# Layer-norm rows in two halves with Newton roots on VectorE, a shift table in four pieces, and a new load order in a single-core convolution-and-MLP kernel

## The chip, the cores and the metric

The kernel runs on one core of a Trainium2 chip. The metric is the device time of one execution in microseconds (us), median of several executions. A core has TensorE (matmuls; PE in the profile, with PEld for its weight loads), VectorE (DVE), ScalarE (ACT), GpSimd (POOL), and the queues of 16 DMA engines (SP starts most loads). They run side by side and wait for each other by semaphores.

Times are compared between kernels run on the same chip in the same set, each with its own executions of the kernel before; where two sets are compared, the text says so, and the kernel before had means of 192.71 to 192.88 us in all of them. That kernel was very steady: 192.63 to 192.95 us in almost all sets (one execution of 193.43).

## The reference

Two branches share the input `q` (2048 rows of 640, bf16), and a gate per row mixes them.

```python
x = A_q                                             # [1, 2048, 640]
g = sigmoid((x * gate_w).sum(-1))                   # gate, one per row
# branch A: 4-tap causal shift of k, times v, then a long convolution along the rows
k_shift = sum over t of k_pad[:, t:t+S, :] * shift_k[:, 3-t]
kv = k_shift * v
y  = irfft(rfft(kv, 2S) * rfft(ssm_k, 2S))[:S] + kv * ssm_D
a  = q * y
# branch B: rows normalised, then an MLP that mixes along the rows
h  = (x - mean(x)) / sqrt(var(x) + 1e-5)            # per row of 640
u  = gelu(einsum("bsd,sf->bdf", h, w1) + b1)
b  = transpose(einsum("bdf,fs->bds", u, w2) + b2)
return g * a + (1 - g) * b
```

## The kernel before

The convolution is done as matrix products with sine tables. The stages that matter here, with the names that tiles have in the program:

1. TensorE transposes the filter (`wT<-ssm`) and transforms it in two blocks of 64 matmuls (`wT,FTB`), "the filter products". ScalarE drains each group of four to `C`. VectorE then combines the result ("filter mixing", `SS<-C`, `C<-C`).
2. VectorE computes mean and variance of 16 tiles of 128 rows (`stats`, `mv`), the reciprocal roots are found (`rstd`), and each tile of `X` is normalised in place.
3. The 4-tap shift of `k` is 80 small matmuls (`KF,KT`) per half against a table `KF` that GpSimd builds: "the k convolution". VectorE multiplies by `v` (`vkv`), TensorE transforms the product (`vkv,FTB`).
4. The first MLP product (`X,ring`, 384 matmuls) needs no branch A. It is the filler that TensorE takes where branch A has nothing ready; every group of it needs normalised rows. The second (`GT,W`) follows, and the inverse transform of branch A (`C,GTB` and `SS,GTB`, four times 32 matmuls) comes between its groups near the end.

The program is written as a list of operations with estimated durations. A list scheduler inside the kernel's own code decides the order on each engine before the program is built, by a priority and those estimates. On the chip the order is fixed; only the waits differ. PSUM is cut in four accumulators: at most three for branch A ("cv") and two for the MLP ("mlp").

```python
self.limit = {"mlp": 2, "cv": 3}          # of NSLOT = 4 accumulators
# ... cut ...
def ln_apply():
    ts("POOL", sd[:, :], mv[:, :, 1], 1e-5, None, ALU.add)               # var + eps
    tt("POOL", rstd[:, :], sd[:, :], V(cst, 1, [[0, 16]]), ALU.pow)      # ** -0.5
    tt("POOL", sd[:, :], sd[:, :], rstd[:, :], ALU.mult)
    for t in range(16):
        xs = X[:, t // 4, t % 4, :]
        ts("DVE", xs, xs, mv[:, t, 0:1], rstd[:, t:t + 1], ALU.subtract, ALU.mult, mode=4, extra=0.16)
# ... cut ...
            if h == 0:
                for hk in range(4):
                    for p in range(4):
                        ln_tile(hk, p)
                ln_apply()
                for g0 in (0, 10):        # the shift table, two pieces
                    tt("POOL", KF[:, g0:g0 + 10, :, :], V(cw, 7 * g0, ...), V(m32, 0, ...), ALU.mult)
                for hk in range(2):
                    k_turn(hk)            # VectorE copies a row block of k, DMA transposes it
                mixing(C[0], SS, 0, fine=True)
```

Of the kernel before, what the change touches and what calls it, by code (L numbers as in the profile page):

```python
# [308 lines left out]
class _Op:  # L309
    __slots__ = ("eng", "dur", "emit", "prio", "idx", "ndep", "succ", "vt", "vtrole", "end", "start", "kind", "lat", "deps", "name", "after", "nafter", "asucc")  # L310

# [11 lines left out]
class _Sched:  # L323
# [29 lines left out]
    def add(self, eng, dur, emit, reads, writes, prio=None, vt=None, lat=0.0, name=""):  # L353
        op = _Op()
        op.eng, op.dur, op.emit, op.lat, op.name = eng, dur, emit, lat, name
        op.idx = len(self.ops)
        op.prio = op.idx if prio is None else prio
        op.vt = vt
        deps = set()
        self._conf(op, reads, "R", deps)  # L360
        self._conf(op, writes, "W", deps)
        if vt is not None:
            vt.left += 1
            if vt.last_pe is not None:
                deps.add(vt.last_pe)
            if eng == "PE":
                if vt.first is None:
                    vt.first = op
                vt.last_pe = op
            else:  # L370
                for d in deps:
                    if d.vt is not vt:
                        if d not in vt.first.deps:
                            vt.first.deps.add(d)
        op.deps = deps
        op.after = set()
        self._rec(op, reads, "R")
        self._rec(op, writes, "W")
        self.ops.append(op)
        return op  # L380

    def run(self):
# [12 lines left out]
        pend = {e: [] for e in engs}  # L395
        free = {e: 0.0 for e in engs}
        dma_free = 0.0
        avail = {}
# [13 lines left out]
        while started < n:  # L412
# [6 lines left out]
            for e in engs:  # L419
# [32 lines left out]
                if e in ("SP", "QA") or op.lat < 0:  # L452
                    issue = 0.1
                    s = max(t + issue, dma_free)
# [3 lines left out]
                else:  # L458
                    op.end = t + op.dur
                    free[e] = op.end  # L460
                order.append(op)
# [43 lines left out]
def _build(nc, A_q, A_k, A_v, A_shift_k, A_ssm_k, A_ssm_D, B_x, B_w1, B_b1, B_w2, B_b2, gate_w, out):  # L505
# [10 lines left out]
    with ExitStack() as es:  # L516
# [97 lines left out]
        def tt(eng, o, a, b, op, mode=2, prio=None):  # L614
            n = n_of(o)
            d = dve_dur(n, mode) if eng == "DVE" else n / 500.0 + 0.3
            return SC.add(eng, d, lambda s: T.op(eng, lambda e: e.tensor_tensor(o, a, b, op), [a, b], [o]),  # L617
                          [a, b], [o], prio=prio, name="tt")

        def ts(eng, o, a, s1, s2, op0, op1=None, mode=1, prio=None, extra=0.0):  # L620
# [4 lines left out]
            def f(e):  # L625
                if s2 is None:
                    return e.tensor_scalar(o, a, s1, None, op0=op0)  # L627
                return e.tensor_scalar(o, a, s1, s2, op0=op0, op1=op1)  # L628
            return SC.add(eng, d, lambda s: T.op(eng, f, rr, [o]), rr, [o], prio=prio, name="ts")

# [89 lines left out]
        def k_turn(hk):  # L720
            o, i = kp[hk % 2], kn[hk % 2]
            ov = o[:, :, :].rearrange("p g (q c) -> p g q c", q=4)
            iv = V(i, 0, [[32, NG], [D, 4], [1, 32]])
            SC.add("DVE", 0.75, lambda s: T.op("DVE", lambda e: e.tensor_copy(ov, iv), [i[:, :, :]], [o[:, :, :]]), [i[:, :, :]], [o[:, :, :]], prio=0, name="kperm")  # L724
            c0 = 16 + 128 * (hk % 2)
# [19 lines left out]
        x_load(0)  # L745
        dma(gwb[:, :], dr(gate_w, 0, [[0, 128], [1, D]]), 128 * 1280, chain=True)
        for hk in range(1, 4):
            x_load(hk)
        ssm_load(2)
        ssm_load(3)  # L750

        T_PI = float(np.float32(math.pi * (1.0 - 1e-6)))
        memset("DVE", cst[:, 0:1], T_PI)
        memset("DVE", cst[:, 1:2], -0.5)
        iota = lambda ap, pat, b, cm: SC.add("POOL", 0.5, lambda s: T.op("POOL", lambda e: e.iota(ap, pat, base=b, channel_multiplier=cm), [], [ap]), [], [ap])
        iota(dif[:, :], [[1, 128]], 0, -1)
# [17 lines left out]
        for hk in range(2):  # L774
            k_load(hk)
        for hk in range(4):
            w1_load(0, hk)

        vt = _VT("cv")
# [41 lines left out]

        def mixing(R, Th, Ts, fine=False, conj=False):
            def sl(h, s, n=1):
# [24 lines left out]

        def ln_apply():
            ts("POOL", sd[:, :], mv[:, :, 1], 1e-5, None, ALU.add)  # L850
            tt("POOL", rstd[:, :], sd[:, :], V(cst, 1, [[0, 16]]), ALU.pow)
            tt("POOL", sd[:, :], sd[:, :], rstd[:, :], ALU.mult)
            for t in range(16):
                xs = X[:, t // 4, t % 4, :]
                ts("DVE", xs, xs, mv[:, t, 0:1], rstd[:, t:t + 1], ALU.subtract, ALU.mult, mode=4, extra=0.16)

        srcW = lambda h: (lambda kt, p, ci: wT[:, 2 * h + kt, p, 320 * ci:320 * ci + 320])
        for h in range(2):
# [5 lines left out]
            if h == 0:  # L864
                for hk in range(4):
                    for p in range(4):
                        ln_tile(hk, p)
                ln_apply()
                for g0 in (0, 10):
                    tt("POOL", KF[:, g0:g0 + 10, :, :], V(cw, 7 * g0, [[7, 10], [1, 7], [0, 32]]), V(m32, 0, [[0, 10], [0, 7], [1, 32]]), ALU.mult)  # L870
                for hk in range(2):
                    k_turn(hk)
                mixing(C[0], SS, 0, fine=True)
            else:
                mixing(C[1], C[0], 0, conj=True)

# [276 lines left out]
```

## Time and profile before

The median is 192.79 us (three executions, 192.77 to 192.95). The profiled execution spans 190.9 us.

| stretch (us) | TensorE | what else |
|---|---|---|
| 0 to 5.34 | waits for the first filter load | |
| 14.29 to 24.55 | 64 filter products, 161 ns each | ScalarE busy 96% |
| 24.55 to 29.2 | 40 transposes, 4.65 us | ScalarE busy throughout |
| 29.2 to 41.8 | 64 filter products and 24 MLP matmuls | |
| 50.3 to 51.75 | waits 1.04 us for the product of k and v | VectorE full |
| 64.6 to 187.8 | 928 matmuls, 132.7 ns each, no gap | |
| 187.8 to 190.9 | done: tail | ScalarE, VectorE, last store |

The first two lines of the page: span and busy times of each engine, with shares and instruction counts.

```profile
span 190.9 us, 3358 instructions
...
PE 177.4 (93%) x1403; PEld 130.5 (68%) x1403; DVE 170.3 (89%) x195; ACT 116.4 (61%) x187; POOL 33.0 (17%) x29
```

TensorE's timeline of the kernel before. Columns: start (us), duration (us), engine, source line (a helper's), operation, output and inputs, shapes, count; in brackets idle time before it and who ended it.

```profile
14.29 10.29 PE L293 MATMUL pp<-wT,FTB 128*128 128x320 bf16 x64 [0.43 <-ACT wT L655]
24.55 0.45 PE L293 MATMUL pp<-ident,ssm 128*128 128x128 bf16 x5
25.15 3.96 PE L293 MATMUL pp<-ident,ssm 128*128 128x128 bf16 x35 [0.15 <-ACT C L655]
29.24 1.31 PE L293 MATMUL pp<-wT,FTB 128*128 128x320 bf16 x8
30.64 1.43 PE L293 MATMUL pp<-X,ring 128*128 128x320 bf16 x8
31.90 4.01 PE L293 MATMUL pp<-wT,FTB 128*128 128x320 bf16 x28
...
40.68 1.25 PE L293 MATMUL pp<-X,ring 128*128 128x320 bf16 x8
41.77 4.33 PE L293 MATMUL pp<-KF,KT 128*128 128x128 bf16 x80
```

Two things are to be seen. The 40 transposes have no MLP group between them, because no row is normalised before 30 us. From 30.64 us on three groups of eight MLP matmuls (`X,ring`) stand inside the second filter block (the first and the last are shown).

Why the rows come at 30 us is in GpSimd's timeline and in VectorE's:

```profile
13.65 7.84 POOL L617 TENSOR_TENSOR KF<-cw,m 128x2240 bf16<-128x2240 bf16 x2 [5.40 <-DVE mv L847]
25.60 1.39 POOL L627 TENSOR_SCALAR sd<-mv 128x16 f32<-128x16 f32 x1 [4.11 <-DVE mv L847]
27.07 2.94 POOL L617 TENSOR_TENSOR rstd<-sd,cst 128x16 f32<-128x16 f32 x1
30.09 0.22 POOL L617 TENSOR_TENSOR sd<-sd,rstd 128x16 f32<-128x16 f32 x1
```

```profile
23.17 1.48 DVE L617 TENSOR_TENSOR SS<-C 128x2560 bf16<-128x2560 bf16 x1
...
30.05 5.79 DVE L628 TENSOR_SCALAR X<-X,mv,rstd 128x640 bf16<-128x640 bf16 x16 [3.19 <-POOL rstd L617]
```

The table runs first, then the roots (1.39 + 2.94 + 0.22 us), and VectorE idles 3.19 us for them. (The page names `mv` as what the table waited for, only because an `mv` ended just before. The table reads `cw` and `m`; ScalarE's drain of `cw` ended at 13.51 us.) The end of TensorE's timeline:

```profile
175.68 4.51 PE L293 MATMUL pp<-SS,GTB 128*128 128x320 bf16 x32
180.02 7.77 PE L293 MATMUL pp<-GT,W 128*128 128x320 bf16 x56
```

After the last inverse product (`SS,GTB`) 56 MLP matmuls follow. The wait of TensorE for the product of k and v, from the list of waits (engine, who waited for whom: total us, times, longest):

```profile
PE pp L293 <- DVE vkv L617: 1.0, 1, 1.0
```

### The profile page before, as it was taken

To read this page: it belongs to the slowest core of one execution; us is meant where nothing else is said; L and a number is where in the kernel's file an instruction comes from. 1 tells how busy PE (TensorE), PEld (TensorE's weight loads), DVE (VectorE), ACT (ScalarE), POOL (GpSimd) and SP (SyncE) were. 2 spreads that over 40 slices of the span, in tenths; PEclk is the share of its full clock that TensorE was granted. 3 is DMA by queue.
4 is the path that set the end of the run, shared out by engine and by line. 5 is a ranking of instruction groups with operands and counts; after the bars stand their busy time and mean duration, and the time that the engine had idled before them with its cause. 6 is when DMAs were issued, how large, how long until landed. Compare 5 with 4: busy or idle time off the path is not lost.

```text
span 190.9 us, 3358 instructions
## 1 busy us (share of the span) xinstructions
PE 177.4 (93%) x1403; PEld 130.5 (68%) x1403; DVE 170.3 (89%) x195; ACT 116.4 (61%) x187; POOL 33.0 (17%) x29
## 2 busy tenths in 40 slices
PE   0749989999799999999999999999999999999993
PEld 0536555678566976767777777888888777886782
DVE  7999967999999799999999969999999958999451
ACT  4799997889599999998411221131322467516632
POOL 2619563600006300010012102250000000000000
PEclk9999999999999999999999999999999999999999
DMA  5999999993799999994368914999947903210222
GB/s 155 327 412 378 372 238 230 307 407 136 136 181 306 250 232 306 272 329 96 59 138 251 231 27 138 272 208 195 263 136 224 367 18 137 72 69 2 72 103 103
DMA packets 37296, 38.93 MB, mean 204 GB/s; under 512 B 15644, under 2 KB 32673, under 8 KB 37281
## 3 DMA queue, kind: packets, MB, share of 16 engines
q1 hardware_dynamic: 34464, 32.15, 54.7%
q0 software_dynamic: 2752, 6.55, 18.6%
q8 instruction: 11, 0.18, 0.4%
q14 instruction: 5, 0.03, 0.0%
q10 hardware_dynamic: 64, 0.01, 0.0%
HBM read 25.87 MB, written 2.62 MB: 149 GB/s over the span
## 4 chain that ended last, share of the span: by engine, by line
PE 71%; DVE 19%; DMA 4%; POOL 2%; issue 2%; SPq 0%; ACT 0%; DVEq 0%
PE pp L293 71%; DVE stats L845 6%; DMA X<-in_A_q_dram 4%; DVE X L628 3%; DVE SS L617 3%; DVE C L617 2%; DVE kp L724 2%; POOL rstd L617 2%; DVE vkv L617 1%; DVE mv L847 1%; POOL sd L627 1%; SPq L267 0%; ACT O L655 0%; DVE O L617 0%; DVEq L187 0%
## 5 line engine op out<-in xcount | busy, mean ns | idle before, releaser
L293 PE MATMUL pp<-X,ring 128*128 128x320 bf16 x384 | 54.0, 299 | 0.1
L293 PE MATMUL pp<-GT,W 128*128 128x320 bf16 x384 | 52.8, 299 | 0.0
L617 DVE TENSOR_TENSOR C<-C 128x2560 bf16<-128x2560 bf16 (+1 forms) x28 | 48.9, 1769 | 1.2 <-ACT C L655 1.1
L293 PEld LDWEIGHTS pp<-GT,W 128*128 128x128 bf16 x384 | 43.5, 113 | 8.9 <-ACT cgb L655 0.2
L293 PEld LDWEIGHTS pp<-X,ring 128*128 128x128 bf16 x384 | 37.1, 98 | 15.4 <-DVE X L628 0.7
L655 ACT ACTIVATE C<-pp 128x640 bf16<-128x640 f32 x64 | 39.6, 741 | 4.4 <-PE pp L293 4.3
L655 ACT ACTIVATE O<-pp,c,omg 128x640 bf16<-128x640 f32 (+1 forms) x17 | 14.5, 853 | 32.9 <-PE pp L293 32.9
L655 ACT ACTIVATE GT<-pp,cc 128x640 bf16<-128x640 f32 x12 | 9.6, 797 | 22.1 <-PE pp L293 21.9
L617 DVE TENSOR_TENSOR tm<-C,C 128x2560 bf16<-128x2560 bf16 (+2 forms) x12 | 20.2, 1708 | 1.9 <-DMA C<-tm 1.9
L293 PE MATMUL pp<-wT,FTB 128*128 128x320 bf16 x128 | 19.6, 310 | 0.6 <-ACT wT L655 0.4
L655 ACT ACTIVATE cgb<-pp,gg 128x640 bf16<-128x640 f32 x16 | 12.7, 793 | 7.7 <-PE pp L293 7.7
L293 PEld LDWEIGHTS pp<-wT,FTB 128*128 128x128 bf16 x128 | 11.5, 101 | 8.0 <-ACT C L655 2.3
L617 DVE TENSOR_TENSOR C<-tm 128x2560 bf16<-128x2560 bf16 (+1 forms) x12 | 15.0, 1263 | 0.1
L293 PE MATMUL pp<-ident,ssm 128*128 128x128 bf16 x80 | 8.8, 265 | 6.6 <-DMA ssm<-in_A_ssm_k_dram 5.3
L262 POOL DMA_DIRECT2D C<-C x6 | 7.5, 1407 | 36.0 <-DVE C L617 36.0
L845 DVE BATCH_NORM_STATS2 stats<-X 128x6 f32<-128x320 bf16 x32 | 13.4, 463 | 0.3 <-DMA X<-in_A_q_dram 0.3
L293 PE MATMUL pp<-C,GTB 128*128 128x320 bf16 x96 | 13.6, 299 | 0.0
L293 PEld LDWEIGHTS pp<-ident,ssm 128*128 128x128 bf16 x80 | 6.3, 127 | 9.1 <-DMA ssm<-in_A_ssm_k_dram 5.3
L293 PEld LDWEIGHTS pp<-C,GTB 128*128 128x128 bf16 x96 | 9.0, 98 | 4.0 <-ACT O L655 0.2
L655 ACT ACTIVATE gq<-gq 128x640 bf16<-128x640 bf16 x16 | 11.8, 756 | 0.0
L617 DVE TENSOR_TENSOR tm<-C,SS 128x5120 bf16<-128x5120 bf16 x4 | 11.2, 2817 | 0.0
L655 ACT ACTIVATE wT<-pp 128x640 bf16<-128x640 f32 x16 | 10.1, 812 | 1.1 <-PE pp L293 1.1
(64 smaller groups left out, 177.2 us busy)
## 6 DMA issues: line engine op xcount, KB each, us to landing
ring<-in_B_w_dram SPq DMA_DIRECT2D x12, 512.0 KB, 10.3
W<-in_B_w_dram SPq DMA_DIRECT2D x8, 768.0 KB, 7.3
C<-C POOLq DMA_DIRECT2D x6, 640.0 KB, 10.5
ssm<-in_A_ssm_k_dram SPq DMA_DIRECT2D x4, 640.0 KB, 9.1
X<-in_A_q_dram SPq DMA_DIRECT2D x4, 640.0 KB, 9.5
kn<-in_A_k_dram SPq DMA_DIRECT2D x4, 640.0 KB, 9.2
out_dram<-O SPq DMA_DIRECT2D x7, 320.0 KB, 2.3
vkv<-in_A_v_dram SPq DMA_DIRECT2D x2, 640.0 KB, 4.7
```

The lines of the kernel that those rows point to most:

```text
L262: ins = engobj.dma_start(out_ap, in_ap, accum_op=ALU.add, max_dma_last_dim=2560)
L293: ins = self.nc.tensor.matmul(ps_ap, lhsT=lhsT, rhs=rhs, start=start, stop=stop, skip_group_check=True)
L617: return SC.add(eng, d, lambda s: T.op(eng, lambda e: e.tensor_tensor(o, a, b, op), [a, b], [o]), [a, b], [o], prio=prio, name="tt")
L627: return e.tensor_scalar(o, a, s1, None, op0=op0)
L628: return e.tensor_scalar(o, a, s1, s2, op0=op0, op1=op1)
L655: return T.op("ACT", lambda e: e.activation(o, src, func, **kw), rr + [src], ww)
L724: SC.add("DVE", 0.75, lambda s: T.op("DVE", lambda e: e.tensor_copy(ov, iv), [i[:, :, :]], [o[:, :, :]]), [i[:, :, :]], [o[:, :, :]], prio ...
L845: SC.add("DVE", 0.38, (lambda o, i: lambda s: T.op("DVE", lambda e: e.bn_stats(o, i), [i], [o]))(o, i), [i], [o])
L847: SC.add("DVE", 0.12, (lambda o, i: lambda s: T.op("DVE", lambda e: e.bn_aggr(o, i), [i], [o]))(o, i), [i], [o])
```

## The change

Its intent: normalise the first eight tiles as soon as their statistics are there, so that MLP matmuls can fill the holes in the first 30 us; take the roots away from GpSimd, where the table stands in the way, and compute them on VectorE by a bit trick and three Newton steps; cut the table in four pieces; give the filter mixing a lower priority; load two pieces of `w1` early. The estimates of the scheduler are corrected as well: operations of VectorE and GpSimd that share a port lock each other in the model.

```diff
+        op.lock = eng == "POOL"            # in the scheduler: such operations wait for one another
+                    if op.lock:
+                        op.end += max(port["POOL" if e == "DVE" else "DVE"] - t, 0.0)
+                        port[e] = op.end
# ... cut: durations of GpSimd operations, lock set on copies and tensor operations ...
         x_load(0)
-        dma(gwb[:, :], ...)
-        for hk in range(1, 4):
-            x_load(hk)
+        x_load(1)
+        w1_load(0, 0)
         ssm_load(2)
         ssm_load(3)
+        x_load(2)
+        w1_load(0, 1)
+        x_load(3)
# ... cut ...
-        def ln_apply():
-            ts("POOL", sd[:, :], mv[:, :, 1], 1e-5, None, ALU.add)
-            tt("POOL", rstd[:, :], sd[:, :], V(cst, 1, [[0, 16]]), ALU.pow)
-            tt("POOL", sd[:, :], sd[:, :], rstd[:, :], ALU.mult)
-            for t in range(16):
+        def ln_scale(a, b):
+            v, y, z, m_ = sd[:, a:b], rstd[:, a:b], gth[:, a:b], mv[:, a:b, 1]
+            # ... cut: yi, vi are y, v read as int32 ...
+                op(lambda e: e.tensor_scalar(v, m_, 1e-5, None, op0=ALU.add), [m_], v)
+                op(lambda e: e.tensor_scalar(yi, vi, 1, None, op0=ALU.logical_shift_right), [vi], yi)
+                op(lambda e: e.tensor_scalar(yi, yi, -1.0, float(0x5F3759DF), op0=ALU.mult, op1=ALU.add), [yi], yi)
+                for _ in range(3):
+                    op(lambda e: e.scalar_tensor_tensor(out=z, in0=y, scalar=-0.5, in1=y, op0=ALU.mult, op1=ALU.mult), [y], z)
+                    op(lambda e: e.tensor_tensor(z, z, v, ALU.mult), [z, v], z)
+                    op(lambda e: e.scalar_tensor_tensor(out=y, in0=z, scalar=1.5, in1=y, op0=ALU.add, op1=ALU.mult), [z, y], y)
+                op(lambda e: e.tensor_tensor(v, v, y, ALU.mult), [v, y], v)
+            return SC.add("DVE", 1.5, emit, [m_], [v, y, z], prio=0, name="rstd")
+        def ln_apply(a, b):
+            for t in range(a, b):
# ... cut ...
+        MIXP = 330
+        LNG = ((0, 8), (8, 16))
+        KFP = (0, 5, 10, 15)
# ... cut ...
+                for a, b in LNG:
+                    for t in range(a, b):
+                        ln_tile(t // 4, t % 4)
+                    ln_scale(a, b)
+                    ln_apply(a, b)
+                for g0 in KFP:              # the shift table, four pieces
+                    tt("POOL", KF[:, g0:g0 + 5, :, :], ...)
-                mixing(C[0], SS, 0, fine=True)
+                mixing(C[0], SS, 0, fine=True, prio=MIXP)
```

More of the change, by code (lines that the diff above doesn't have):

```diff
@@ L309 @@
 class _Op:
-    __slots__ = ("eng", "dur", "emit", "prio", "idx", "ndep", "succ", "vt", "vtrole", "end", "start", "kind", "lat", "deps", "name", "after", "nafter", "asucc")
+    __slots__ = ("eng", "dur", "emit", "prio", "idx", "ndep", "succ", "vt", "vtrole", "end", "start", "kind", "lat", "deps", "name", "after", "nafter", "asucc", "lock")
 class _VT:
@@ L396, in run @@
         free = {e: 0.0 for e in engs}
+        port = {"DVE": 0.0, "POOL": 0.0}
         dma_free = 0.0
@@ L452, in run @@
                 if e in ("SP", "QA") or op.lat < 0:
-                    issue = 0.1
+                    issue = 1.2 if e == "POOL" else 0.1
                     s = max(t + issue, dma_free)
@@ L615, in tt @@
             n = n_of(o)
-            d = dve_dur(n, mode) if eng == "DVE" else n / 500.0 + 0.3
-            return SC.add(eng, d, lambda s: T.op(eng, lambda e: e.tensor_tensor(o, a, b, op), [a, b], [o]),
-                          [a, b], [o], prio=prio, name="tt")
+            d = dve_dur(n, mode) if eng == "DVE" else n / 600.0 + 0.17
+            o_ = SC.add(eng, d, lambda s: T.op(eng, lambda e: e.tensor_tensor(o, a, b, op), [a, b], [o]),
+                        [a, b], [o], prio=prio, name="tt")
+            o_.lock = True
+            return o_
+        tt_ = tt
         def ts(eng, o, a, s1, s2, op0, op1=None, mode=1, prio=None, extra=0.0):
@@ L628, in f @@
                 return e.tensor_scalar(o, a, s1, s2, op0=op0, op1=op1)
-            return SC.add(eng, d, lambda s: T.op(eng, f, rr, [o]), rr, [o], prio=prio, name="ts")
+            o_ = SC.add(eng, d, lambda s: T.op(eng, f, rr, [o]), rr, [o], prio=prio, name="ts")
+            o_.lock = eng == "POOL" or mode > 1
+            return o_
         def stt(eng, o, a, sc, b, op0, op1, acc=None, prio=None):
@@ L723, in k_turn @@
             iv = V(i, 0, [[32, NG], [D, 4], [1, 32]])
-            SC.add("DVE", 0.75, lambda s: T.op("DVE", lambda e: e.tensor_copy(ov, iv), [i[:, :, :]], [o[:, :, :]]), [i[:, :, :]], [o[:, :, :]], prio=0, name="kperm")
+            SC.add("DVE", 0.75, lambda s: T.op("DVE", lambda e: e.tensor_copy(ov, iv), [i[:, :, :]], [o[:, :, :]]), [i[:, :, :]], [o[:, :, :]], prio=0, name="kperm").lock = True
             c0 = 16 + 128 * (hk % 2)
@@ L745, in _build @@
         x_load(0)
-        dma(gwb[:, :], dr(gate_w, 0, [[0, 128], [1, D]]), 128 * 1280, chain=True)
-        for hk in range(1, 4):
-            x_load(hk)
+        x_load(1)
+        w1_load(0, 0)
         ssm_load(2)
         ssm_load(3)
+        x_load(2)
+        w1_load(0, 1)
+        x_load(3)
         T_PI = float(np.float32(math.pi * (1.0 - 1e-6)))
@@ L754, in _build @@
         memset("DVE", cst[:, 1:2], -0.5)
-        iota = lambda ap, pat, b, cm: SC.add("POOL", 0.5, lambda s: T.op("POOL", lambda e: e.iota(ap, pat, base=b, channel_multiplier=cm), [], [ap]), [], [ap])
+        iota = lambda ap, pat, b, cm: SC.add("POOL", 0.2, lambda s: T.op("POOL", lambda e: e.iota(ap, pat, base=b, channel_multiplier=cm), [], [ap]), [], [ap])
         iota(dif[:, :], [[1, 128]], 0, -1)
@@ L775, in _build @@
             k_load(hk)
-        for hk in range(4):
+        for hk in range(2, 4):
             w1_load(0, hk)
+        dma(gwb[:, :], dr(gate_w, 0, [[0, 128], [1, D]]), 128 * 1280, chain=True)
         vt = _VT("cv")
@@ L820, in fwd, with mixing, tt @@
                     act(o, two, ACT.Copy, vt=vt, name=name + "e", **kw)
-        def mixing(R, Th, Ts, fine=False, conj=False):
+        def mixing(R, Th, Ts, fine=False, conj=False, prio=None):
+            def tt(*a):
+                return tt_(*a, prio=prio)
             def sl(h, s, n=1):
@@ L847, in ln_tile, with emit, op @@
             SC.add("DVE", 0.12, (lambda o, i: lambda s: T.op("DVE", lambda e: e.bn_aggr(o, i), [i], [o]))(o, i), [i], [o])
-        def ln_apply():
-            ts("POOL", sd[:, :], mv[:, :, 1], 1e-5, None, ALU.add)
-            tt("POOL", rstd[:, :], sd[:, :], V(cst, 1, [[0, 16]]), ALU.pow)
-            tt("POOL", sd[:, :], sd[:, :], rstd[:, :], ALU.mult)
-            for t in range(16):
+        def ln_scale(a, b):
+            v, y, z, m_ = sd[:, a:b], rstd[:, a:b], gth[:, a:b], mv[:, a:b, 1]
+            yi = y.bitcast(I32)
+            vi = v.bitcast(I32)
+            def emit(s):
+                def op(fn, rr, w):
+                    T.op("DVE", fn, rr, [w])
+                op(lambda e: e.tensor_scalar(v, m_, 1e-5, None, op0=ALU.add), [m_], v)
[9 more added lines that the diff above has]
+            for t in range(a, b):
                 xs = X[:, t // 4, t % 4, :]
-                ts("DVE", xs, xs, mv[:, t, 0:1], rstd[:, t:t + 1], ALU.subtract, ALU.mult, mode=4, extra=0.16)
+                ts("DVE", xs, xs, mv[:, t, 0:1], rstd[:, t:t + 1], ALU.subtract, ALU.mult, mode=4, extra=0.16, prio=1)
+        MIXP = 330
+        LNG = ((0, 8), (8, 16))
+        KFP = (0, 5, 10, 15)
         srcW = lambda h: (lambda kt, p, ci: wT[:, 2 * h + kt, p, 320 * ci:320 * ci + 320])
@@ L864, in _build @@
             if h == 0:
-                for hk in range(4):
-                    for p in range(4):
-                        ln_tile(hk, p)
-                ln_apply()
-                for g0 in (0, 10):
-                    tt("POOL", KF[:, g0:g0 + 10, :, :], V(cw, 7 * g0, [[7, 10], [1, 7], [0, 32]]), V(m32, 0, [[0, 10], [0, 7], [1, 32]]), ALU.mult)
+                for a, b in LNG:
[4 more added lines that the diff above has]
+                for g0 in KFP:
+                    tt("POOL", KF[:, g0:g0 + 20 // len(KFP), :, :], V(cw, 7 * g0, [[7, 20 // len(KFP)], [1, 7], [0, 32]]), V(m32, 0, [[0, 20 // len(KFP)], [0, 7], [1, 32]]), ALU.mult)
                 for hk in range(2):
                     k_turn(hk)
-                mixing(C[0], SS, 0, fine=True)
+                mixing(C[0], SS, 0, fine=True, prio=MIXP)
             else:
-                mixing(C[1], C[0], 0, conj=True)
+                mixing(C[1], C[0], 0, conj=True, prio=MIXP)
         memset("POOL", KT[0][:, :, 15:16], 0.0)
```

## The prediction

> **What bounds the kernel now.** The stretches show TensorE busy 177.4 of 190.9 us; the chain of waits is 71% TensorE, one unbroken run from 51.75 to 187.8 us. From 64.6 us it takes 123.2 us for 928 matmuls (132.7 ns each): saturated, so the only gain there is having less left to do. The tail (3.1 us) and the wait for the first filter load (5.3 us) are untouched. Holes between 18 and 65 us:
> - 24.55 to 29.2: 40 filter transposes take 4.65 us (113 ns each; ScalarE drains five per 0.63 us). The short matmuls of the k convolution go at 54 ns, so 2.4 us are free.
> - 14.3 to 24.55: 64 filter matmuls at 161 ns instead of 133, again paced by ScalarE; about 0.6 us free after 20 us.
> - 29.2 to 41.8: 88 matmuls in 12.6 us, 0.85 us free.
> - 46 to 51.75: TensorE waits 1.04 us for the k·v product, which on VectorE stood behind the filter mixing.
> - 51.75 to 64.6: about 0.7 us.
>
> Sum 5 to 6 us, the ceiling. The filler is the first MLP product, which needs normalised rows, now from about 30.5 us: statistics end at 25.5 us, GpSimd then needs 1.39 + 2.94 + 0.22 us for the roots, and VectorE idles 3.2 us.
>
> **What the change does.**
> - Halves: statistics of 8 tiles, 8 x 0.86 us (8.8 to 15.7); Newton, 13 dependent small operations at an estimated 0.15 to 0.2 us (independent ones show 0.17), 2 to 2.6 us; then 8 x 0.36 us. First rows at about 18 us, half done at 21 to 24; second half at 34 to 36, as before (35.8).
> - VectorE pays two Newton chains (4 to 5 us) and saves 3.2 us of idling: about even.
> - Half the rows and two MLP accumulators give at most 32 matmuls, 4.3 us of filler: just what the holes before 34 us take.
> - The shift table on GpSimd (2 x 3.9 us from 13.65) now overlaps the normalising. The Trainium skill ("SBUF — State Buffer", on the shared port pair) says such VectorE instructions and GpSimd ones lock each other out for a whole instruction. The trace agrees: GpSimd's 16-element add took 1.39 us, ending with VectorE's 1.45 us operation. Four pieces keep each block to about 2 us.
> - With the mixing behind, k·v goes first: most of the 1.04 us goes. The last inverse products have 7.8 us of MLP matmuls behind them as slack.
> - Two weight pieces go earlier, so k and the last rows land about 2.8 us later (1 MB at 370 GB/s), at 19 to 24 us; VectorE gets to them no earlier.
>
> **Predicted time.** Of the 5 to 6 us, 3 to 4 should be won: 2 to 2.5 in the transposes and first filter products, 0.8 in the k·v wait, the rest small. 189.5 us, 8 in 10 between 187.6 and 191.5; faster by over 2% 0.32, within 2% 0.66, slower 0.02.
>
> **What would show it.** MLP matmuls in TensorE's timeline from 18 to 22 us, between transposes; the stretch of transposes over 95% useful; no wait on k·v above 0.3 us; the saturated run starting some 3 us earlier with as much left; the tail still 3.1 us; VectorE busy some 3 us more; first-half normalising instructions that last 1 to 2 us where a table piece runs.
>
> **What would make it wrong.** Table pieces that block the first half beyond 24 us; Newton steps twice as dear; MLP groups that give ScalarE, over 90% busy before 42 us, bubbles; k transposes that land late and starve the k convolution; deferred mixing that makes inverse products late near 150 or 171 us.

## The result, and the profile after

The changed kernel took 193.62 us (median of four executions), the kernel before 192.78 us. The ratio is 1.004 (95% interval 1.002 to 1.006): within 2%, but slower, where 189.5 us were predicted. Three of the four executions took 193.45 to 193.70 us. One, the profiled one, took 1038.88 us and is left out; it is told of at the end.

Because of that the profile shown is of a later execution of the same kernel (the run e9 below, 193.32 us). Its page:

```profile
span 191.5 us, 3379 instructions
...
PE 177.3 (93%) x1403; PEld 129.9 (68%) x1403; DVE 180.4 (94%) x221; ACT 116.3 (61%) x187; POOL 26.6 (14%) x28
```

TensorE's busy time is the same to 0.1 us. VectorE's went up by 10.1 us, not by some 3. VectorE's timeline where the roots are computed, and the table on GpSimd beside it:

```profile
16.04 0.94 DVE L874 TENSOR_SCALAR sd<-mv 128x8 f32<-128x8 f32 x1
17.01 1.99 DVE L875 TENSOR_SCALAR rstd<-sd 128x8 int32<-128x8 int32 x1
19.03 1.99 DVE L876 TENSOR_SCALAR rstd<-rstd 128x8 int32<-128x8 int32 x1
21.05 1.98 DVE L878 SCALAR_TENSOR_TENSOR gth<-rstd 128x8 f32<-128x8 f32 x1
23.07 0.17 DVE L879 TENSOR_TENSOR gth<-gth,sd 128x8 f32<-128x8 f32 x1
...
24.75 2.94 DVE L637 TENSOR_SCALAR X<-X,mv,rstd 128x640 bf16<-128x640 bf16 x8
```

```profile
14.88 8.13 POOL L622 TENSOR_TENSOR KF<-cw,m 128x1120 bf16<-128x1120 bf16 x4 [6.62 <-ACT cw L666]
```

This is the first thing to see. An operation on eight columns takes 0.17 us when nothing stands beside it (the fifth line). The first four took 0.94, 1.99, 1.99 and 1.98 us, and they end, one for one, as the four pieces of the table end (at 16.94, 18.97, 20.99 and 14.88 + 8.13 = 23.01 us; the fifth operation starts at 23.07). The Newton chain took 8.7 us (16.04 to 24.75) instead of the predicted 2 to 2.6. The Trainium skill ("SBUF — State Buffer", section "Who interferes with whom") says that a VectorE instruction in a two-port mode, or with two inputs in SBUF, contends with a GpSimd instruction that reads SBUF, and that the second to issue blocks fully until the first ends. The trace agrees, down to operations of eight columns. It also agrees with what the same section says of instructions outside these cases: the statistics ran at 0.46 us each beside the table, in both kernels.

VectorE's timeline of the second half:

```profile
35.87 1.48 DVE L622 TENSOR_TENSOR SS<-C 128x2560 bf16<-128x2560 bf16 x1
...
37.38 1.49 DVE L622 TENSOR_TENSOR C<-C 128x2560 bf16<-128x2560 bf16 x1
...
41.30 1.49 DVE L622 TENSOR_TENSOR SS<-C 128x2560 bf16<-128x2560 bf16 x1
42.70 2.94 DVE L637 TENSOR_SCALAR X<-X,mv,rstd 128x640 bf16<-128x640 bf16 x8
```

The second half is normalised from 42.70 to 45.6 us; before, all 16 tiles were done at 35.84. Three mixing operations stand in front, though the change wanted them behind. TensorE's timeline for the same stretch as above:

```profile
13.86 10.46 PE L293 MATMUL pp<-wT,FTB 128*128 128x320 bf16 x64
24.29 0.44 PE L293 MATMUL pp<-ident,ssm 128*128 128x128 bf16 x5
25.34 1.43 PE L293 MATMUL pp<-X,ring 128*128 128x320 bf16 x8 [0.61 <-DVE X L637]
26.60 1.00 PE L293 MATMUL pp<-ident,ssm 128*128 128x128 bf16 x15
27.44 1.25 PE L293 MATMUL pp<-X,ring 128*128 128x320 bf16 x8
...
29.76 0.47 PE L293 MATMUL pp<-ident,ssm 128*128 128x128 bf16 x5 [0.24 <-ACT wT L666]
30.36 9.67 PE L293 MATMUL pp<-wT,FTB 128*128 128x320 bf16 x64
39.99 4.33 PE L293 MATMUL pp<-KF,KT 128*128 128x128 bf16 x80
```

The first MLP group comes at 25.34 us, not at 18 to 22, after a wait of 0.61 us for rows. Two groups (16 matmuls) stand between the transposes, and none in the second filter block: the third group belongs to the same accumulator and needs the second half's rows. So the filler came earlier, but there were 16 matmuls of it before the k convolution where there had been 24. Two waits of TensorE remain:

```profile
PE pp L293 <- DVE vkv L622: 0.6, 1, 0.6
PE pp L293 <- DVE X L637: 0.6, 1, 0.6
```

And the end:

```profile
180.55 1.79 PE L293 MATMUL pp<-GT,W 128*128 128x320 bf16 x12
182.18 4.51 PE L293 MATMUL pp<-SS,GTB 128*128 128x320 bf16 x32
```

Here nothing follows the last inverse product. TensorE ends at 186.7 us, 1.1 us before the old kernel's 187.8, but the tail is 4.8 us (191.5 - 186.7) instead of 3.1 (190.9 - 187.8).

The account between the two traces: TensorE is 1.1 us ahead from 51 us on (it starts its product of k and v at 50.64 instead of 51.75, with the same work done), stays so to its end, and the tail gives back 1.7 us.

### The profile page after: what moved, and what is told of

It reads as the page before. It is cut to its first block, busy times and chain, and to the rows that moved or that the text cites. A ratio compares the mean times of both kernels' runs of the same rounds, so it can differ in the third digit from the quotient of the medians.

```text
span 1037.1 us, 3379 instructions
## 1 busy us (share of the span) xinstructions
PE 1026.6 (99%) x1403; PEld 438.7 (42%) x1403; DVE 177.1 (17%) x221; ACT 125.4 (12%) x187; POOL 27.5 (3%) x28
## 3 DMA queue, kind: packets, MB, share of 16 engines
q1 hardware_dynamic: 34464, 32.15, 10.1%
## 4 chain that ended last, share of the span: by engine, by line
PE 99%; DMA 0%; DVE 0%; ACT 0%; DVEq 0%; issue 0%
PE pp L293 99%; DMA ssm<-in_A_ssm_k_dram 0%; DVE cgb L622 0%; ACT cgb L666 0%; DVE O L622 0%; DVEq L503 0%
## 5 line engine op out<-in xcount | busy, mean ns | idle before, releaser
L293 PE MATMUL pp<-X,ring 128*128 128x320 bf16 x384 | 320.3, 1212 | 0.0
L293 PE MATMUL pp<-GT,W 128*128 128x320 bf16 x384 | 318.6, 1211 | 0.0
L293 PEld LDWEIGHTS pp<-GT,W 128*128 128x128 bf16 x384 | 123.8, 323 | 193.4 <-issue 193.4
L293 PEld LDWEIGHTS pp<-X,ring 128*128 128x128 bf16 x384 | 124.0, 323 | 189.5 <-issue 187.4
L293 PE MATMUL pp<-wT,FTB 128*128 128x320 bf16 x128 | 106.5, 1213 | 0.0
L293 PE MATMUL pp<-C,GTB 128*128 128x320 bf16 x96 | 80.4, 1209 | 0.0
L293 PE MATMUL pp<-vkv,FTB 128*128 128x320 bf16 x64 | 54.1, 1204 | 0.0
L293 PE MATMUL pp<-kv,FTB 128*128 128x320 bf16 x64 | 53.9, 1210 | 0.0
L293 PE MATMUL pp<-KF,KT 128*128 128x128 bf16 (+1 forms) x160 | 47.0, 663 | 0.0
L293 PEld LDWEIGHTS pp<-KF,KT 128*128 128x128 bf16 x160 | 43.5, 314 | 5.0 <-issue 2.1
```

The lines of the kernel that those rows point to most:

```text
L293: ins = self.nc.tensor.matmul(ps_ap, lhsT=lhsT, rhs=rhs, start=start, stop=stop, skip_group_check=True)
```

## The experiments

Two theories stood at the start. Theory L/P: the table blocks the Newton chain piece by piece (P), and VectorE's lateness sets the time (L). Rival T: TensorE is full from 64 us on and VectorE has slack, so its lateness costs nothing; then the loss has another cause. Theory E came from the first traces: the order at TensorE's end makes the tail. Theory S came later: the late second half starves the filler.

| run | what differs from the changed kernel | median us | ratio to before (95%) |
|---|---|---|---|
| first | nothing | 193.62 | 1.004 (1.002 to 1.006) |
| e0 | nothing | 194.44 | 1.008 (1.004 to 1.012) |
| e9 | nothing | 193.80 | 1.006 (1.004 to 1.007) |
| e1 | one Newton step | 192.31 | 0.998 (0.995 to 1.000) |
| e2 | table in two pieces (TensorE's order moved a little) | 194.41 | 1.009 (1.007 to 1.010) |
| e3, e11 | table behind the first half | 192.22, 192.21 | 0.998, 0.997 |
| e10 | 12 MLP matmuls last on TensorE | 193.03 | 1.001 (0.997 to 1.004) |
| e12 | as e11, inverse product last | 193.57 | 1.005 (1.003 to 1.006) |
| e16 | table behind, every order kept | 192.01 | 0.996 (0.994 to 0.997) |
| e17 | e16 and e10 together | 190.91 | 0.989 (0.988 to 0.991) |
| e13 | as e11, mixing really behind (other orders moved too) | 191.06 | 0.991 (0.989 to 0.992) |
| e4 | table behind, roots on GpSimd | 191.68 | 0.994 (0.993 to 0.996) |
| e5 | as e4, second MLP accumulator early | 195.95 | 1.015 (1.012 to 1.019) |
| e6 | load order of before | 192.12 | 0.996 (0.994 to 0.998) |
| e7 | table behind, Newton not in halves | 195.60 | 1.015 (1.012 to 1.018) |
| e8 | e4 with the load order of before | 191.55 | 0.993 (0.990 to 0.996) |
| e14 | e8 with the mixing behind | 191.80 | 0.995 (0.993 to 0.997) |
| e15 | e14 with Newton roots | 191.58 | 0.996 (0.994 to 0.998) |

All gave correct results.

### e0: the changed kernel again

No edit.

> The changed kernel unchanged, because its profiled execution took 1038.9 us with matmuls of 1.2 us each, while its three other executions took 193.45 to 193.70. Theory A (that execution was disturbed from outside the program): this look takes 193.5 us within 0.3 and its matmuls of 320 columns are back to about 0.30 us each. Theory B (the changed program has a slow mode of its own): one of its executions here again takes over 250 us. The trace should also show why it is 0.8 us slower than before and not 3.3 us faster: either TensorE fills the transposes before 29 us and loses elsewhere before 65 us, or its first MLP matmul comes later than 22 us.

Measured: 194.44 us (193.82 to 195.22), matmuls of 320 columns at 0.30 us. So the 1038.9 us were of that one execution; it did not come back in the 10 executions of e0 and e9, and the profiles above and below could be read. The expectation of 193.5 within 0.3 us missed: this kernel spreads. The traces of e0 (195.02 us) and e9 (193.32 us) show where these two differ: in e0 TensorE waited 1.25 us at 145 us for a load of `w2`, in e9 not. The first filter block took 11.6 us in e0 and 10.5 in e9, but that was nearly made up by shorter waits for VectorE after it: at the second k convolution e0 is only 0.25 us behind (61.62 against 61.37). The line of e0:

```profile
146.03 17.04 PE L293 MATMUL pp<-GT,W 128*128 128x320 bf16 x124 [1.25 <-DMA W<-in_B_w_dram]
```

### e1: one Newton step instead of three

```diff
-                for _ in range(3):
+                for _ in range(1):
```

Its result is a little less exact. The scheduler does not see inside the chain, so every engine's order stays.

> One Newton step instead of three in each half, order of everything else on every engine the same: VectorE has 12 operations of about 0.2 us less, 2.4 us in all; the result is a little less exact, on purpose. Theory L (VectorE's lateness sets the end of the changed kernel): 1 to 2.5 us faster than the changed kernel's 193.5 to 195.2, and the first MLP matmul about 1.2 us earlier, at 24.7 us. Rival T (TensorE sets the end, full from 64 us on, and VectorE has slack as the prediction held): no change within 0.4 us. The blocked steps remain: the first four Newton operations still take 0.9 + 3 x 2 us.

Measured: 192.31 us, ratio 0.998 against 1.004 to 1.008 for the changed kernel: 1.2 to 1.9 us for 12 small operations that take 2.4 us on VectorE. The first four operations were still blocked (0.88, 1.99, 1.99, 1.98 us). First MLP matmul at 25.28 us, hardly earlier, since the filter block before it ran until 25.0 in this trace; what went are the waits for rows and for the product of k and v. Rival T falls: VectorE's lateness counts. But it counts through waits of TensorE before 51 us, not at the end as theory L had it: the tail is still 4.8 us.

### e2: the table in two pieces

```diff
-        KFP = (0, 5, 10, 15)
+        KFP = (0, 10)
```

> The shift table in two pieces of about 4 us, as before, in place of four of 2 us. Theory P (each small VectorE operation waits for one whole GpSimd piece, one after another): two Newton operations of up to 4 us, chain over only when the table is done, at about 23.3 us plus the rest, first rows normalised again near 25 us and the time within 0.5 us of the changed kernel. Rival Q (the long operations are a cost of the first integer or shift operation, not of GpSimd): still three operations of 2 us each. Prediction (shorter pieces block less): four pieces would be better, so this one is 2 us or more later at the first rows.

Measured: 194.41 us, within the spread of four pieces. (The new estimates also moved a few of TensorE's groups between 65 and 81 us, and a wait of 0.68 us for VectorE stands there, so the time alone is no clean measure. The chain is.) VectorE's timeline of this run:

```profile
16.00 2.78 DVE L874 TENSOR_SCALAR sd<-mv 128x8 f32<-128x8 f32 x1
18.81 3.87 DVE L875 TENSOR_SCALAR rstd<-sd 128x8 int32<-128x8 int32 x1
22.72 0.17 DVE L876 TENSOR_SCALAR rstd<-rstd 128x8 int32<-128x8 int32 x1
```

Two operations are blocked, of 2.78 and 3.87 us, and the chain is free at 22.7 us. Theory P holds and Q falls. Two pieces or four make no difference to this chain: it pays until the table is done, one operation for each piece. By the trace the next piece has started before the next operation of the chain is issued.

### e3: the table behind the first half

```diff
-                    tt("POOL", KF[...], V(cw, ...), V(m32, ...), ALU.mult)
+                    # the same, with one read more: X[:, 1, 3, :], the last row tile of the first half,
+                    # so that a semaphore makes the table wait for it
```

> The shift table must wait for the first half's normalised rows (it reads the last of them as a dependency), so that nothing runs on GpSimd beside the Newton chain. Theory P/L: Newton 13 x 0.2 = 2.6 us, first rows at about 19 us instead of 25, VectorE's last products 5 to 6 us earlier, first MLP matmul at 20 to 23 us, time 1.5 to 3.5 us below the changed kernel: 190.5 to 192. Rival T: first rows earlier, time the same within 0.5 us. The table itself may now collide with the row copies of k on VectorE.

Measured: 192.22 us. The chain took 2.5 us, normalising began at 18.6 us, the first MLP group stands at 21.8 us. But the scheduler had also put 12 MLP matmuls behind the last inverse product. Two causes were mixed, which e9 to e12 and e16, e17 take apart. The table now ran beside VectorE's row copies of k, which took 1.66 and 2.22 us instead of 0.82.

### e4: roots back on GpSimd, in halves, table behind

```diff
+            ts("POOL", v, m_, 1e-5, None, ALU.add)
+            tt("POOL", y, v, V(cst, 1, [[0, b - a]]), ALU.pow)
+            tt("POOL", v, v, y, ALU.mult)
-            # the 13 VectorE operations
```

> Halves kept, but the roots back on GpSimd (add, power, product), the table behind the first half. VectorE is freed of 2 x 2.6 us of Newton and of 6 us of blocking, and can take statistics of the second half during the first roots. Theory L: faster than the table-behind kernel with Newton by 1 to 3 us, 188.5 to 190.5, and faster than before. If the power takes 2.9 us for 8 columns as for 16, first rows come at about 19.5 us. Rival T: the same as the table-behind kernel within 0.5 us.

Measured: 191.68 us, faster than before (0.994). It is 0.4 us below e3 by the mean, but the executions overlap (191.34 to 191.85 against 191.39 to 192.43) and TensorE's order differs too, so rival T's "the same within 0.5 us" stands here; the expected 188.5 to 190.5 was too bold. VectorE is busy 172.4 us instead of 176.5. The power of eight columns took 1.68 us.

### e5: the second accumulator early

```diff
-                mms(vt, items, prio=10 ** 6 + 4 * ft + hk, name="m1")
+                mms(vt, items, prio=(150 if ft < 2 and hk < 2 else 10 ** 6 + 4 * ft + hk), name="m1")
```

> As the kernel with roots on GpSimd and the table behind, but the MLP's second row block is let into a second accumulator early, so that 32 MLP matmuls and not 16 stand before the second filter block, as the prediction assumed. Theory F (the filler was too little: one accumulator, 16 matmuls): TensorE reaches the second k convolution about 2 us earlier than that kernel's 60.7 us for the same work and the time falls by 1 to 2 us, to 189.7 to 190.7. Rival G (ScalarE paces that stretch whatever TensorE does, and the inserted matmuls only delay its drains): the same within 0.5 us or slower.

Measured: 195.95 us against e4's 191.68. TensorE's timeline in the second filter block of this run:

```profile
36.16 1.31 PE L293 MATMUL pp<-wT,FTB 128*128 128x320 bf16 x8 [0.20 <-ACT C L666]
```

Eight filter products take 1.51 us (36.16 to the next at 37.67), with such a wait in each pair of groups; in e9 the same block goes at 1.21 us for eight (9.67 us for 64). With two accumulators held by the MLP, branch A has two instead of three, and ScalarE's drains are no longer hidden. The prediction's 32 early MLP matmuls were to be had, but at a loss of 4.3 us. Theory F falls, and the rival holds more strongly than it was put.

### e6: the load order of before

```diff
-        # the change's order: x0 x1 w1(0) ssm2 ssm3 x2 w1(1) x3
+        # x0 gate x1 x2 x3 ssm2 ssm3, w1 after k
```

> The changed kernel with the load order of before, all else as changed. The blocking of the Newton chain by the table stays, so first rows again at about 25 us. If the early weight pieces matter, first MLP matmuls are later; but the list order also changes: 24 MLP matmuls end up behind the last inverse product instead of none. Theory E (the tail of 4.8 us comes from the inverse product standing last on TensorE): tail back to about 3.1 us and the time 1 to 2 us below the changed kernel's 193.5 to 194.4. Rival: the tail stays long because VectorE is late, time unchanged.

Measured: 192.12 us. The first rows come at 23.4 us, since the table began earlier (13.2 us) and met three operations of the chain, not four. 24 MLP matmuls stand last, and the tail is 3.1 us, as theory E expected. The orders and the blocking changed with the loads, so this time does not say what the load order is worth; e8 against e4 does.

### e7: no halves

```diff
-        LNG = ((0, 8), (8, 16))
+        LNG = ((0, 16),)
```

This is e3 with one Newton chain for all tiles.

> Newton on VectorE for all 16 tiles at once, no halves, table behind the first half's rows. Nothing is blocked. Roots at about 23 us plus 2.6 us, first rows near 26 us instead of 19, all rows by 32 to 34 us instead of 42. VectorE saves one chain of 2.6 us. If halves are what helps, this is slower than the table-behind kernel with halves (192.2) by 0.5 us or more; if the late second half is what hurts there, it is the same or faster. Its inverse product stands last on TensorE, so theory E expects a tail of 4.8 us here.

Measured: 195.60 us, and inconclusive about halves. The table, waiting for rows that now come at 34 us, ran from 37.2 to 47.6 us beside row copies (4.1 us for two) and normalising (5.0 us for four tiles), and the k convolution waited for it. It shows again what the port costs, not what halves give. Its inverse product stands last.

### e8: roots on GpSimd with the load order of before

The edits of e4 and e6 together.

> Load order of before, halves, roots on GpSimd, table behind the first half; 24 MLP matmuls behind the last inverse product. Nothing blocked, tail 3.1 us. Expected at or below the same with the new load order (191.7): 190.5 to 191.7; a gain over that would say that the early weight pieces cost more than they give.

Measured: 191.55 us, equal to e4 (191.68, another chip) within the spread: with the orders that the scheduler makes for each, the early weight pieces neither cost nor give a measurable time.

### e9 to e12: two by two on one chip

The kernel e10 holds the last MLP group behind the last inverse product; e12 does the opposite to e11.

```diff
         inverse(0, Z0)
+        inv_ = [o for o in SC.ops if o.name == "inv"][-1]
+        [o for o in SC.ops if o.name == "m2"][-1].after.add(inv_)      # e10: only an edge of order
```

> The changed kernel again, on the same chip as the next three, as their reference: 193.5 to 195. Two by two: table beside the Newton chain or behind it, last inverse product or 12 MLP matmuls last on TensorE.

> The changed kernel with one thing altered: its last 12 MLP matmuls stand behind the last inverse product (32 matmuls) and not before it; one drain on ScalarE moves with them, every other order is the same. Theory E (order of the end): tail after the last matmul 3.1 to 3.2 us in place of 4.8, time 1.2 to 1.8 us below the reference of this set. Rival (VectorE's lateness, not the order, makes the end late): TensorE then waits for the last product before those 32 matmuls, in the trace about 1 us or more, and the time falls by less than 0.6 us.

> Table behind the first half, 12 MLP matmuls last, as run before at 192.2. If blocking costs by itself, it is 0.5 us or more below the changed kernel with the same end (the run before this one); if its gain came only from the end, the two are equal within 0.3 us.

> Table behind the first half, but the last inverse product last, as in the changed kernel. Theory E: 1.2 to 1.8 us slower than the run before this one, tail 4.8 us. Against the changed kernel of this set (same end) it shows what the blocking alone costs: theory P expects 0.5 to 2 us, the rival nothing beyond 0.3 us.

Mean times in us (six executions each):

| | inverse product last | 12 MLP matmuls last |
|---|---|---|
| table beside the Newton chain | 193.87 (e9) | 192.97 (e10) |
| table behind the first half | 193.64 (e12) | 192.20 (e11) |

The end's order is worth 0.9 us in the first row and 1.4 us in the second. The tails in the traces are 3.2 us (e10, e11) against 4.8 (e9, e12). Nothing of VectorE's was late in e10: TensorE went into the last inverse product without a wait. Theory E holds; the gain of e10 is below the expected 1.2 us, and its profiled execution has the wait of 1.3 us for `w2` again. The table's place seems to be worth only 0.2 and 0.8 us. But e11 and e12 also have another order of TensorE between 65 and 81 us, and after 160 us: from the first of the 32 MLP matmuls at 65 us to the long run of them e9 takes 15.3 us, e11 and e12 take 15.8. So the column is no clean measure; e16 and e17 below give one.

### e13: the mixing really behind

The change gives the mixing priority 330. Built with and without that, the program is the same, instruction for instruction (a repeated build gave two identical programs), so this part of the change does nothing. In the scheduler's own list of start times a mixing operation of 1.4 us starts whenever VectorE is free for the 0.08 us that the scheduler allows for a statistics result to arrive. An order edge does what the priority does not:

```diff
+                last_rows = [o for o in SC.ops if o.name == "ts"][-1]
                 mixing(C[0], SS, 0, fine=True, prio=MIXP)
+                # for each of its operations: o.after.add(last_rows)
```

> Table behind the first half (the 192.2 kernel), and the first filter's mixing held behind the last normalised row of the second half by an order edge, which the priority of the change does not do: with or without that priority the built program is the same, and three mixing operations of 1.48 us ran before the second half's rows. Theory S (the late second half starves the filler: 16 MLP matmuls stand before the first k convolution, 24 did in the kernel before): rows of the second half done at about 37.5 us instead of 41.7, 24 MLP matmuls before that k convolution, time 0.3 to 1 us below 192.2. Rival: no change within 0.3 us, since the mixing's lateness is paid later.

Measured: 191.06 us, mean 190.97 against 192.20 for e11 (another chip): 1.2 us. TensorE's timeline of the second filter block:

```profile
29.98 7.28 PE L293 MATMUL pp<-wT,FTB 128*128 128x320 bf16 x48
37.10 1.25 PE L293 MATMUL pp<-X,ring 128*128 128x320 bf16 x8
38.18 2.34 PE L293 MATMUL pp<-wT,FTB 128*128 128x320 bf16 x16
40.37 4.33 PE L293 MATMUL pp<-KF,KT 128*128 128x128 bf16 x80
```

The rows of the second half were done at 37.8 us instead of 41.8 (e3, the same program as e11), a third MLP group stands inside the block (at 37.10 us), and 24 matmuls stand before the k convolution. So the edge does what it should, but the 1.2 us cannot be put down to theory S. The edge also moved TensorE's order between 65 and 81 us back to that of e9, and its order after 160 us. The trace of e3, whose first filter block is as long as that of e13 (11.26 us), shows where the 1.3 us between the two lie: at 61 us e13 is 8 MLP matmuls (1.1 us) ahead and 0.7 us later, so some 0.4 us; 0.4 us more come between 65 and 81 us (15.35 against 15.77) and 0.5 us after 115 us. And e17 below, with its second half done at 42.4 us and 16 matmuls before the k convolution, is as fast as e13 (190.85 and 190.97, two chips). That the late second half costs time is not shown.

### e14 and e15: the same on the old load order

The edge of e13 added to e8 (e14), and with the Newton roots in place of the power (e15).

> All that helped so far together: load order of before, halves, roots on GpSimd, table behind the first half, mixing behind the second half, 12 MLP matmuls after the last inverse product. 40 MLP matmuls stand before the end of the first k convolution. Theory S: 190 to 191.2, at least 0.4 us below the same without the mixing edge (191.5). Rival: 191.3 or more.

> As the last one, but with the roots by Newton on VectorE, unblocked; TensorE's order is the same in both, so the difference is what VectorE's 26 small operations cost, 5.2 us of VectorE less 2 x 2 us of waiting for GpSimd's roots: 0 to 1 us slower than the last one, if VectorE's lateness still counts.

Measured: 191.80 and 191.58 us, no better than e8 (191.55). Here theory S's gain does not show. The order had moved again: the k convolution was cut in two with an MLP group between, and before its second part (at 45.93 us in e14) TensorE waits 0.46 us for ScalarE. So this is no clean test of the second half's lateness either. Newton or power makes no difference when nothing blocks (means 191.86 and 191.84).

### e16 and e17: only the blocking, every order kept

The scheduler is told the same times as in the changed kernel, so that each engine's order is that of the changed kernel to the last operation, and the table waits for the first half as in e3. e17 adds the edge of e10.

```diff
+                    # the table reads X[:, 1, 3, :] as in e3, and takes no lock in the scheduler
-    ... mode=4, extra=0.16, prio=1)
+    ... mode=4, extra=0.16 + {0: 1.455, 1: 2.035}.get(t, 0.0), prio=1)     # estimates only
```

> The changed kernel with the same order of operations on every engine, and one dependency more: the table on GpSimd waits for the first half's last normalised row. So nothing differs but the blocking. One Newton step instead of three, the other run at equal order, gave 1.2 to 2.1 us for 2.4 us less on VectorE. Theory P: the chain takes 2.6 us, the waits of TensorE for rows and for the k and v product (0.6 us each in the reference trace) go, 1 to 1.5 us below the changed kernel (ratio to before 1.0057), so a ratio of 0.998 to 1.000. Rival (the two by two's small difference is all): 0.2 to 0.8 us, ratio 1.001 to 1.005.

> The last one with the 12 MLP matmuls behind the last inverse product: another 0.9 to 1.4 us, ratio to before 0.992 to 0.995, and so about 0.5 us faster than the earlier kernel with the table behind, whose orders had also shifted between 65 and 81 us (ratio 0.9971).

Measured: e16 192.01 us, mean 191.96; e17 190.91 us, mean 190.85. The traces of e9 and e16 have the same list of operations on every engine, and those of e10 and e17 too. Against e9 (193.87, another set, where the kernel before had the same mean of 192.78 us) the blocking alone costs 1.9 us, more than expected, and 2.1 us between e10 and e17 (192.97 and 190.85). The end's order costs another 1.1 us (e16 to e17; 0.9 from e9 to e10). These four are the clean two by two. The 1.9 us are net of what the moved table costs elsewhere: the row copies of k beside it take 2.00 and 1.50 us in e16 instead of 0.82. VectorE's timeline of e16:

```profile
16.24 0.17 DVE L874 TENSOR_SCALAR sd<-mv 128x8 f32<-128x8 f32 x1
...
18.76 2.93 DVE L637 TENSOR_SCALAR X<-X,mv,rstd 128x640 bf16<-128x640 bf16 x8
```

and TensorE's end in e17:

```profile
180.09 4.51 PE L293 MATMUL pp<-SS,GTB 128*128 128x320 bf16 x32
184.44 1.79 PE L293 MATMUL pp<-GT,W 128*128 128x320 bf16 x12
```

The chain takes 2.5 us, and the two waits of TensorE of 0.6 us are gone. In the traces TensorE is 1.3 us ahead of e9 at the second k convolution (60.07 against 61.37 us) and 0.9 at its end, after a wait for `w2` in e16. The traced execution of e9 (193.32 us) was its fastest and that of e16 (192.41) its slowest, so the traces show less than the means. e17 is the fastest kernel beside e13: 1.1% below the kernel before.

## Why the prediction was wrong

The aim of the change and the place of the gain were right: TensorE is saturated after 64 us, the filler comes earlier, and the wait for the product of k and v fell (1.04 to 0.61 us, 0 without the blocking). The size was wrong, and so was the sign. Point by point:

- "Four pieces keep each block to about 2 us." Each block was 2 us, and there were four of them, because the prediction counted the pieces against normalising and forgot that the Newton operations before it take the port too. The half was done at 27.7 us, not at 21 to 24. This is the term that failed first: Newton 2 to 2.6 us, measured 8.7. Its cost in the end is 1.9 us (e16). The prediction's own list of what would make it wrong begins with this ("block the first half beyond 24 us"). The change makes the same mistake in code: its scheduler gets a lock for tensor operations and copies, but the Newton chain is entered with 1.5 us and without the lock.
- "The last inverse products have 7.8 us of MLP matmuls behind them as slack." That was read from the old order. The scheduler made a new one with none behind. "The tail still 3.1 us" was 4.8. Cost 0.9 to 1.1 us at equal order (e10, e17). The prediction treated the order as fixed, though it is computed anew from every estimate that the change touches.
- "Second half at 34 to 36, as before." It was 42.7 to 45.6. Blocking made part of it (without it the half is done at 42.5 us, e16); the mixing in front of it made another (37.8 us without both, e13), though the prediction believed "with the mixing behind". That part of the change is without effect. That it costs time is not shown: e13 was 1.2 us below e11, but other orders moved with it, e17 is as fast as e13 with the half as late as in e16, and e14 gained nothing.
- "Half the rows and two MLP accumulators give at most 32 matmuls." It was 16, and 32 are worse (e5): there the third accumulator of branch A is worth more.
- "VectorE busy some 3 us more": 10.1 us more. Of this the blocking is 6.2 us (8.7 - 2.5), the rest is about the Newton operations themselves (26 of 0.17 us).
- "Normalising instructions in the first half that last 1 to 2 us": none; the lock fell on the chain before them.

The first two are shown, alone and together: with both mended (e17) the mean falls from 193.87 to 190.85 us, 3.0 of the 4.4 us by which the prediction was below e9. The other 1.4 us stay open.

What also stays open is part of the spread of these kernels. The load of `w2` was reached 1.25 to 1.33 us too early in e0 and e10, 0.17 us in e16 and not at all in e9; why it lands later in some executions was not followed. The first filter block takes 10.5 to 11.7 us in six traces of the same order, and for that the traces have a cause. Its first matmuls start 267 ns apart and last about 0.47 us, the others start 136 ns apart and last 0.30 us. The first kind are 9 of 64 in e9 (block 10.46 us), 11 in e16 (10.69), 13 in e10 (10.88), 15 in e1 (11.17), 19 in e0 (11.59) and 19 in e17 (11.65). Where the blocked VectorE is waited for anyway, this is nearly absorbed (e0 and e9 above); without the blocking it is not: e17 starts the second k convolution 0.85 us after e16. The kernel before has 8 of the first kind, so the 161 ns that the prediction put down to ScalarE are in part this.

## What to carry to other kernels

Before moving a chain of small dependent operations from GpSimd to VectorE, look at what GpSimd will run beside it: here each of them waited for one whole GpSimd instruction, so cutting that work in pieces did not help, and making it wait did. Where an order is computed by a scheduler from estimates, a change of estimates moves work far away from the change; compare the order at the end of the bound engine first, and check that each part of a change alters the program at all. To compare two traces, count the filler matmuls up to the same milestone, and before a gain is put down to an edit, check that the scheduler left every other order as it was: e13 looked like a clean gain of 1.2 us and was not.

## What the Trainium skill lacked or had wrong

- "SBUF — State Buffer", section "Who interferes with whom", has the lock right, and its rule that the first to issue wins, but does not tell what becomes of a chain: between two dependent small VectorE operations GpSimd starts its next instruction, so that four pieces cost 0.94 + 1.99 + 1.99 + 1.98 us (e9) and two pieces 2.78 + 3.87 us (e2).
- "GPSIMD Engine Reference" has no time for a power. It took 2.94 us for 16 columns of 128 partitions (the kernel before) and 1.68 us for 8 (fp32, e4), and 2.75 us for 8 with VectorE's tensor operations beside it (e4, second half).
- "TensorE: Matmul & The Clock Gate" (Part 1) says that matmuls run at half the clock until the engine has been busy for a window of about 3.4 us that runs freely. It is not wrong here, though a look at the profile alone can make it seem so. The first filter block goes at 267 ns for each matmul of 320 columns and then at 136; the change comes 2.4 us (e9) to 5.1 us (e17) after the block begins. The row of the granted clock shows 1.00 before it as well, but the trace's list of granted clocks has no entry there: its first, at full clock, begins at 16.30 us in e9 and 19.08 us in e0, just where the matmuls become faster.
- None has a case like the execution of 1038.9 us: the 384 matmuls of the second MLP product took 318.6 us of TensorE (0.83 us each, 6 times the usual 0.1375), while VectorE was busy 177.1 us, no more than usual. The 1.0 given for its clock is no measurement, since its page has no row of the granted clock. The nearest is a caveat of "TensorE: Matmul & The Clock Gate" (Part 1), that the clock has been seen held at a quarter for over 50 us; a factor of 6 through a whole execution is not there. It was one execution of more than 80 of these kernels, and its cause is open. The line of its page (busy us, then mean ns of one):

```profile
L293 PE MATMUL pp<-GT,W 128*128 128x320 bf16 x384 | 318.6, 1211 | 0.0
```
